# One feature multiply per tile on GpSimd instead of three on two engines, with VectorE's order fixed by the plan

## The chip, the cores and the metric

One core of one Trainium2 chip. The time is device microseconds (us) of one execution; a kernel's figure is the median of its runs. Engines are named as in the profile: PE is TensorE, DVE is VectorE, ACT is ScalarE, POOL is GpSimd, SP is the engine that issues the DMAs. Each profile is of a single execution.

All runs are called fast by the rule used here (not over 1.5% above the fastest of the same kernel). Inside that there are two groups for the kernel before: in the three sets of experiments 11 of its 33 runs took 276.15 to 276.73 us, ten of them with a mean granted PE clock of 0.994, the rest about 274.1 us. In the second set six of the eleven were of the longer kind, so that its median for the kernel before is 276.15 us. Where a few tenths matter I compare medians of runs with a clock of 0.999 or 1.0, and lengths inside the traces.

## The reference, cut to what matters

```python
def reference(A_x, A_wqkv, A_w_phi, A_wo, B_x, B_w1, B_w3, B_w2):   # x: 1 x 2048 x 640, bf16
    xn = _layernorm(A_x)                                            # H = 32 heads of 20
    return A_x + _A_ref(xn, ...) + _B_ref(xn, ...)

# _A_ref: linear attention. phi of q and of k is the pair of soft maxima of +p and -p:
    pk = jnp.einsum("bhsd,hdf->bhsf", k, w_phi)
    phi_k = jnp.concatenate([_softmax(pk), _softmax(-pk)], axis=-1)   # the same for q
    kv = einsum(phi_k, v);  num = einsum(phi_q, kv);  den = einsum(phi_q, sum of phi_k)
    out = (num / den) @ wo
# _B_ref: gated MLP, (silu(x w1) * (x w3)) w2, with 1536 hidden columns
```

## The kernel before

The 2048 rows are 16 tiles of 128. A tile of keys or queries becomes features in four steps: PE projects, ACT takes the exponentials of +p and -p (1280 numbers per row), DVE sums each head's 20 numbers and takes 64 reciprocals, and then the exponentials are multiplied by them into `phi`. The 32 heads are laid out in 11 blocks of three, so the last block has two heads. The kernel before multiplies the ten full blocks on POOL, one instruction for each sign, and the two heads left over on DVE:

```python
        def red():                                     # DVE: sums per head
            nc.vector.reduce_sum(out=box["s"]..., in_=box["e"]..., axis=AX.X)
        def rec():                                     # DVE: 64 reciprocals
            nc.vector.reciprocal(out=box["r"][:], in_=box["s"][:])
        n = HB * (NB - 1)                              # 30 of the 32 heads
        def tail():                                    # DVE: the last two heads, 80 numbers
            pinned[key, t] = nc.vector.tensor_mul(out=box["phi"][:, NB - 1, :, 0 : 2 * Dh]..., 
                in0=box["e"][:, :, n * Dh : D]..., in1=box["r"][:, :, n:H, None].to_broadcast(...))
        for sgn, eng in enumerate(engines):            # POOL, twice 600 numbers
            def mul(sgn=sgn, eng=eng): ...
```

All work is first entered in a `Plan`, a list scheduler in Python with a guessed duration for each operation. It puts the operations in order of their planned start. In the kernel before, the instructions are then handed over in that order, but the scheduler of the tile framework may still reorder them on each engine. Two things tie it down: the DMA queue is chained, and "pins" place the layer norm's statistics and applies on DVE behind a named instruction:

```python
    for h in parts:
        ins = nc.vector.bn_stats(out=stats[:, t, h, :], in_=xg[c][:, i, ...])
        if k is not None:
            order_after(ins, pinned[k])
```

The gated MLP runs in the gaps: for each of 48 groups PE does two sets of five 128x512 matmuls into PSUM banks (six in the ring), ACT takes `th = tanh(gate/2)`, DVE forms `gs = (th + 1) * gate`, ACT copies `up`, POOL multiplies `hT = gs * up`. A gate bank is free for PE again only when DVE has done `gs`.

The softmax here doesn't subtract the row's maximum and nothing guards it: scores larger than these inputs give would overflow.

## Time and profile before

274.14 us, median of 5 (273.95 to 274.28).

| what | value | where read |
|---|---|---|
| span of the trace | 272.6 us | page |
| PE busy | 264.4 us, 97% | page |
| PE waits in the middle | 0.80, 0.52, 0.76, 0.94 us | timeline of PE |
| DVE busy | 184.7 us, 68% | page |
| small multiplies on DVE | 32, together 27.8 us | groups by form |

The head of the page of the kernel before: span, then for each engine busy time, share and number of instructions.

```profile
span 272.6 us, 5218 instructions
...
PE 264.4 (97%) x1964; PEld 163.8 (60%) x1964; DVE 184.7 (68%) x347; ACT 127.0 (47%) x285; POOL 138.9 (51%) x154
...
```

PE is busy 97% of the time, so little is left to win: 8 us, and the start and the end own some of that. The list of waits of PE (who waited, for whom: total us, times, longest):

```profile
...
PE bank L633 <- DVE gs L654: 2.1, 3, 0.8
PE bank L432 <- DMA wv<-in_A_wqkv_dram: 1.2, 1, 1.2
PE kva L562 <- DVE phi L517: 0.9, 1, 0.9
...
PE bank L406 <- DVE xn L339: 0.3, 1, 0.3
```

The first and third lines are the ones a change in the middle of the kernel can win. The table of windows in four stretches of 10 us (busy time and count of PE, PE weight loads, DVE, ACT, POOL; then clock, DMA share, GB/s):

```profile
...
40.00:50.00 10.00, 9.20 (x56) 4.64 (x55) 9.90 (x16) 5.80 (x13) 8.27 (x8) 1.00 0.84 229
50.00:60.00 10.00, 9.48 (x78) 5.59 (x77) 8.42 (x17) 6.21 (x14) 9.67 (x10) 1.00 0.30 101
...
90.00:100.00 10.00, 10.00 (x86) 6.77 (x85) 10.00 (x12) 7.37 (x20) 6.42 (x6) 1.00 0.01 2
100.00:110.00 10.00, 9.24 (x66) 5.50 (x64) 10.00 (x11) 6.66 (x17) 7.62 (x7) 1.00 0.65 196
...
```

DVE is full in two of the stretches where PE stops for it, 40:50 and 100:110. But it is as full in 90:100, where PE does not stop, and in 50:60, where PE stops at 53.3 us, it is busy for only 8.42 of 10 us. So a full DVE alone does not tell where PE stops. The groups by form (output and inputs, shapes, count, then busy us and mean ns of one), first of DVE, then of POOL:

```profile
...
L507 DVE TENSOR_TENSOR phi<-eq,qr 128x80 bf16<-128x80 bf16 x16 | 15.0, 939 | 0.2
...
L339 DVE TENSOR_SCALAR xn<-xg,mv,rstd 128x640 bf16<-128x640 bf16 x16 | 12.8, 806 | 0.1
L507 DVE TENSOR_TENSOR phi<-ek,kr 128x80 bf16<-128x80 bf16 x16 | 12.8, 799 | 0.3
...
```

```profile
...
L517 POOL TENSOR_TENSOR phi<-eq,qr 128x600 bf16<-128x600 bf16 x32 | 37.8, 1203 | 23.7 <-DVE qr L501 18.7 <-issue 2.5 <-ACT eq L481 2.4
...
```

An 80-element multiply at 0.80 to 0.94 us is dear beside a 600-element one at 1.2 us on POOL.

### The profile page before, as it was taken

The numbers are of one execution on the slowest core, as the hardware profiler recorded it, in microseconds if no ns is written. First come the engines' busy times: TensorE is split into PE (matmuls) and PEld (weight loads), VectorE is DVE, ScalarE is ACT, GpSimd is POOL, SyncE is SP. The second block draws the span as 40 slices with busy tenths as digits, with TensorE's granted clock in tenths as the row PEclk, the third lists the DMA queues.
The fourth block names the chain that finished last, engine by engine and source line by source line (L and its number), as shares of the span: only waits on it lengthen the run. The fifth ranks groups of instructions, "written<-read, shape, count | busy, mean of one in ns | idle before, by whom it ended". The sixth has DMA issues, their size and how long they took to land.

```text
span 272.6 us, 5218 instructions
## 1 busy us (share of the span) xinstructions
PE 264.4 (97%) x1964; PEld 163.8 (60%) x1964; DVE 184.7 (68%) x347; ACT 127.0 (47%) x285; POOL 138.9 (51%) x154
## 2 busy tenths in 40 slices
PE   7999999899999998999989999999999999999996
PEld 2545555455555665666645577766665765657775
DVE  5525899976866999799997828876567563444321
ACT  3668676557667776677754404233234133121000
POOL 6133567994568576988885422434632553112000
PEclk9999999999999999999999999999999999999999
DMA  7999917700260016706169456299815747312241
GB/s 199 311 246 296 269 52 176 266 2 0 96 99 0 2 54 180 216 24 173 69 165 333 111 140 167 103 230 277 209 49 140 173 145 202 101 51 63 83 73 48
DMA packets 70265, 38.11 MB, mean 140 GB/s; under 512 B 49632, under 2 KB 68192, under 8 KB 70240
## 3 DMA queue, kind: packets, MB, share of 16 engines
q1 hardware_dynamic: 69664, 37.42, 51.1%
q10 hardware_dynamic: 576, 0.36, 0.5%
q8 instruction: 15, 0.25, 0.4%
q14 instruction: 10, 0.08, 0.1%
HBM read 12.81 MB, written 12.98 MB: 95 GB/s over the span
## 4 chain that ended last, share of the span: by engine, by line
PE 77%; DVE 13%; issue 4%; DMA 2%; ACT 2%; SPq 0%; ACTq 0%; DVEq 0%
PE bank L633 30%; PE bank L798 19%; PE bank L432 16%; PE bank L811 8%; DVE xn L339 2%; DVE ks L490 2%; DVE phi L507 2%; DMA wv<-in_A_wqkv_dram 2%; PE rtbank L708 2%; DVE gs L654 2%; DVE qs L490 2%; DVE stats L294 1%; PE bank L590 1%; DVE kr L501 1%; ACT ek L481 1%
## 5 line engine op out<-in xcount | busy, mean ns | idle before, releaser
L633 PE MATMUL bank<-xnT,w 128*128 128x512 bf16 x480 | 110.1, 379 | 2.1 <-DVE gs L654 2.1
L677 POOL TENSOR_TENSOR hT<-gs,up 128x512 bf16<-128x512 bf16 x48 | 56.1, 1171 | 77.1 <-DVE gs L654 35.2
L633 PEld LDWEIGHTS <-w 128*128 128x128 bf16 x480 | 46.4, 98 | 52.4 <-issue 2.8
L432 PEld LDWEIGHTS <-xnT 128*128 128x128 bf16 x480 | 45.8, 98 | 21.3 <-issue 1.2
L798 PE MATMUL bank<-w,hT 128*128 128x320 bf16 (+2 forms) x396 | 55.0, 295 | 0.0
L517 POOL TENSOR_TENSOR phi<-eq,qr 128x600 bf16<-128x600 bf16 x32 | 37.8, 1203 | 23.7 <-DVE qr L501 18.7
L798 PEld LDWEIGHTS <-hT 128*128 128x128 bf16 x396 | 38.2, 98 | 15.6
L649 ACT ACTIVATE th<-bank 128x512 bf16<-128x512 f32 x48 | 28.7, 599 | 39.8 <-PE bank L633 39.8
L654 DVE SCALAR_TENSOR_TENSOR gs<-th,bank 128x512 bf16<-128x512 bf16 x48 | 32.5, 678 | 19.7 <-ACT th L649 19.2
L481 ACT ACTIVATE eq<-bank 128x320 bf16<-128x320 f32 x64 | 22.9, 439 | 44.1 <-PE bank L432 33.7
L672 ACT ACTIVATE up<-bank 128x512 bf16<-128x512 f32 x48 | 28.7, 597 | 24.9 <-PE bank L633 24.9
L517 POOL TENSOR_TENSOR phi<-ek,kr 128x600 bf16<-128x600 bf16 x31 | 37.0, 1213 | 0.0
L490 DVE TENSOR_REDUCE qs<-eq 128x64 f32<-128x1280 bf16 x16 | 23.7, 1482 | 12.0 <-ACT eq L481 12.0
L490 DVE TENSOR_REDUCE ks<-ek 128x64 f32<-128x1280 bf16 x16 | 23.6, 1472 | 8.7 <-ACT ek L481 8.7
L432 PE MATMUL bank<-wv,xnT 128*128 128x320 bf16 x160 | 24.7, 299 | 1.3 <-DMA wv<-in_A_wqkv_dram 1.2
L811 PE MATMUL bank<-wo,oT 128*128 128x320 bf16 (+2 forms) x165 | 24.6, 294 | 0.0
L432 PE MATMUL bank<-wkphi,xnT 128*128 128x320 bf16 x160 | 24.3, 299 | 0.0
L432 PE MATMUL bank<-wqphi,xnT 128*128 128x320 bf16 x160 | 24.3, 299 | 0.0
L737 DVE TENSOR_SCALAR den<-rtbank 128x18 f32<-128x18 f32 (+1 forms) x32 | 4.9, 173 | 27.8 <-PE rtbank L708 27.8
L481 ACT ACTIVATE ek<-bank 128x320 bf16<-128x320 f32 x64 | 23.0, 439 | 0.6 <-PE bank L432 0.4
L825 DVE TENSOR_TENSOR res<-bank,xr 128x320 bf16<-128x320 f32 (+2 forms) x33 | 14.5, 470 | 10.4 <-PE bank L811 10.4
L811 PEld LDWEIGHTS <-oT 128*128 128x128 bf16 x165 | 14.9, 97 | 4.9
(55 smaller groups left out, 188.1 us busy)
## 6 DMA issues: line engine op xcount, KB each, us to landing
pqd<-phi SPq DMA_DIRECT2D x16, 352.0 KB, 2.7
w<-in_B_w_dram SPq DMA_DIRECT2D x8, 480.0 KB, 7.0
xr<-in_A_x_dram SPq DMA_DIRECT2D x4, 640.0 KB, 6.9
od<-om SPq DMA_DIRECT2D x16, 160.0 KB, 2.5
out_dram<-res SPq DMA_DIRECT2D x15, 160.0 KB, 2.3
xnd<-xn SPq DMA_DIRECT2D x3, 640.0 KB, 3.2
w<-in_B_w_dram SPq DMA_DIRECT2D x1, 1920.0 KB, 8.4
xg<-in_A_x_dram SPq DMA_DIRECT2D x9, 160.0 KB, 3.5
```

Source lines behind the costliest of these rows:

```text
L432: nc.tensor.matmul(o["ps"][:], xnT[:, c, t * P : (t + 1) * P], w[:, c, 320 * half : 320 * half + 320], start=(c == 0), stop=(c == KD - 1),)
L481: nc.scalar.activation(out=box["e"][:, sgn, 320 * half : 320 * half + 320], in_=o["ps"][:], func=AF.Exp, scale=1.0 - 2.0 * sgn,)
L490: nc.vector.reduce_sum(out=box["s"][:].rearrange("p a h -> p (a h)"), in_=box["e"][:].rearrange("p a (h d) -> p (a h) d", d=Dh), axis=AX.X,)
L517: (nc.vector if eng == "DVE" else nc.gpsimd).tensor_mul(out=box["phi"][:, 0 : NB - 1, sgn, 0 : HB * Dh].rearrange("p b (h d) -> p b h d", ...
L633: nc.tensor.matmul(o["ps"][:], w[:, k, fi * P : (fi + 1) * P], xs[:, k, :], start=(k == 0), stop=(k == KD - 1))
L649: nc.scalar.activation(out=box["th"][:], in_=og["ps"][:], func=AF.Tanh, scale=0.5)
L654: pinned["g", c, fi] = nc.vector.scalar_tensor_tensor(out=box["gs"][:], in0=box["th"][:], scalar=1.0, in1=og["ps"][:], op0=ALU.add, op1=AL ...
L672: nc.scalar.activation(out=box["up"][:], in_=ou["ps"][:], func=AF.Copy, scale=0.5)
L677: lambda: nc.gpsimd.tensor_mul(out=hT[c][:, fi, :], in0=box["gs"][:], in1=box["up"][:]),
L798: nc.tensor.matmul(o["ps"][:], hT[c][:, fi, ti * P : (ti + 1) * P], w2[:, fi, lo:hi], start=(fi == 0), stop=False,)
L811: nc.tensor.matmul(o["ps"][:], oT[c][:, k, ti * P : (ti + 1) * P], wo_of[0][:, k, lo:hi], start=False, stop=(k == KD - 1),)
L825: nc.vector.tensor_tensor(out=box["res"][:, lo:hi], in0=o["ps"][:], in1=xr[c][:, ti, lo:hi], op=ALU.add)
```

## The change

Its intent: take work off DVE, let the plan know that DVE and POOL can block each other, and make DVE follow the plan exactly.

- Exponentials and reciprocals get padded buffers with zeros (33 heads instead of 32), so one POOL instruction of 1320 elements makes a whole `phi`; the small DVE multiply is gone. Key tiles 14 and 15 are multiplied wholly on DVE.
- The plan gets a shared `port`: POOL's operations and some of DVE's queue behind one another in it.
- The pins go; DVE and SP (not PE, ACT and POOL) are held to the planned order (`manual_schedule`).
- Query tile 6 moves between the last two key accumulations; read-outs and residual loads move a little; five warm-up matmuls in place of two at one point.
- Some guesses of the plan change as well: the second block of x is expected at 24.5 instead of 19 us, some durations differ, and `gs` and a few others get a head start (`soon`).

The diff, cut to its core:

```diff
+            done = (max(t, port) if o["port"] else t) + o["dur"]        # Plan.run
+            if o["port"]:
+                port = done
...
+    exps = [acts.tile([P, 2, HB * NB, Dh], bf, name=f"exp{i}") for i in range(4)]
+    recs = [acts.tile([P, 2, HB * NB], f32, name=f"rec{i}") for i in range(2)]
...
-        muls.append(plan.op("DVE", dve_us(2 * (H - n) * Dh), tail, deps=[last, pa], frees=[ea]))
-        for sgn, eng in enumerate(engines): ...                      # two of 600 on POOL
+        if engines == ("DVE", "DVE"):
+            muls = [plan.op("DVE", dve_us(1320), mul(0, 2, nc.vector), ..., port=True)]
+        elif engines[1] == "POOL":
+            muls = [plan.op("POOL", 2.5, mul(0, 2, nc.gpsimd), deps=[last, pa], frees=[ea])]
...
-        ... features(t, "k", ("POOL", "POOL" if t < NST - 1 else "DVE"))
+        ... features(t, "k", ("POOL", "POOL") if t < NST - 2 else ("DVE", "DVE"))
...
-                if k is not None:
-                    order_after(ins, pinned[k])
...
-    plan.op("PE", 0.4, lambda: dummies(2))
+    plan.op("PE", 0.4, lambda: dummies(5))
...
-        if 8 <= t < 15:
+        if 8 <= t < 14:
             Q(t - 8)
     KV(NST - 2)
+    Q(6)
...
-    for o in order: ... order_after(ins, queued)                     # SP only
+    with tc.manual_schedule(engines={ET.SP, ET.DVE}):
+        for o in order:
+            if o["n"] >= early:
+                o["fn"]()
```

More of the change, by code (lines that the diff above doesn't have):

```diff
@@ L17, in __init__, with op @@
         self.ops = []
-    def op(self, eng, dur, fn, deps=(), takes=None, frees=(), after=0.0, lat=0.0, soon=0.0):
+    def op(self, eng, dur, fn, deps=(), takes=None, frees=(), after=0.0, lat=0.0, soon=0.0, port=False):
         o = dict(eng=eng, dur=dur, fn=fn, deps=[d for d in deps if d is not None], takes=takes,
-                 frees=list(frees), after=after, lat=lat, soon=soon, n=len(self.ops), end=None, open=0)
+                 frees=list(frees), after=after, lat=lat, soon=soon, port=port or eng == "POOL", n=len(self.ops), end=None, open=0)
         for f in o["frees"]:
@@ L36, in run @@
         left = len(self.ops)
+        port = 0.0
         def ready(o):
@@ L66, in run @@
                 ring.remove(min(ring))
-            o["start"], o["end"] = t, t + o["dur"] + o["lat"]
-            free[o["eng"]] = t + o["dur"]
+            done = (max(t, port) if o["port"] else t) + o["dur"]
+            if o["port"]:
+                port = done
+            o["start"], o["end"] = t, done + o["lat"]
+            free[o["eng"]] = done
             queue[o["eng"]].remove(o)
@@ L247, in kv_constants @@
             nc.gpsimd.memset(phi[:, :, :, HB * Dh : 64], 0.0)
-            nc.gpsimd.memset(phi[:, NB - 1, :, 2 * Dh : HB * Dh], 0.0)
+        for e in exps:
+            nc.gpsimd.memset(e[:, :, H:, :], 0.0)
+        for r in recs:
+            nc.gpsimd.memset(r[:, :, H:], 0.0)
         for q in range(2):
@@ L253, in kv_constants @@
         )
-    pinned = {}
     pin_of = {}
-    def order_after(ins, other):
-        tc.add_manual_dep(
-            ins.ins, other.ins.name,
-            mybir.DependencyInfo(mybir.DependencyClass.NoSync, mybir.DependencyReason.DATA), reason="order",
-        )
     plan = Plan(dict(bank=6, five=4, half=2, pair=4, phi=5, om=4, kv=2, th=3, gs=3, up=3, hT=3, big=3))
@@ L277 @@
     rstd = consts.tile([P, NST], f32, name="rstd")
-    arrive = [2.2, 2.6, 3.0, 3.4] + [19.0] * 4
+    arrive = [2.2, 2.6, 3.0, 3.4] + [24.5] * 4
     stats_of = {}
@@ L293, in fn @@
             for h in parts:
-                ins = nc.vector.bn_stats(out=stats[:, t, h, :], in_=xg[c][:, i, h * 320 : (h + 1) * 320])
-                if k is not None:
-                    order_after(ins, pinned[k])
+                nc.vector.bn_stats(out=stats[:, t, h, :], in_=xg[c][:, i, h * 320 : (h + 1) * 320])
             if parts[-1] == 1:
@@ L338, in fn @@
         def fn():
-            ins = nc.vector.tensor_scalar(
+            nc.vector.tensor_scalar(
                 out=xn[c][:, i, :], in0=xg[c][:, i, :], scalar1=mv[:, t, 0:1], scalar2=rstd[:, t : t + 1],
@@ L342, in fn @@
             )
-            if k is not None:
-                order_after(ins, pinned[k])
-        apply_of[t] = plan.op("DVE", 0.5, fn, deps=[rstd_of[t], *deps], frees=[xg_of[c]])
+        apply_of[t] = plan.op(
+            "DVE", dve_us(D, 4), fn, deps=[rstd_of[t], *deps], frees=[xg_of[c]], port=True, soon=1.5 if c == 1 else 0.0
+        )
         return apply_of[t]
@@ L369, in LN_out @@
             "SP", 0.5,
-            lambda: [nc.sync.dma_start(out=xn_d[c][:].rearrange("(t p) d -> p t d", p=P), in_=xn[c][:])],
+            lambda: nc.sync.dma_start(out=xn_d[c][:].rearrange("(t p) d -> p t d", p=P), in_=xn[c][:]),
             deps=ds, frees=[a], lat=3.5,
@@ L374, in tr @@
         def tr():
-            pinned["xnT", c] = ins = nc.sync.dma_start_transpose(
+            nc.sync.dma_start_transpose(
                 out=xnT[:, :, 512 * c : 512 * c + 512], in_=xn_d[c][:]
             )
-            return [ins]
         xt = plan.op("SP", 2.5, tr, deps=[st], lat=3.0)
@@ L462, in features @@
         box = {}
-        exps = []
+        done = []
         w, ready = (wkphi, wphi_ready["k"]) if key == "k" else (wqphi, wphi_ready["q"])
         def al():
-            box["e"] = work.tile([P, 2, D], bf, name="e" + key, tag="pair", bufs=4)
+            box["e"] = exps.pop(0)
+            exps.append(box["e"])
         def alp():
@@ L481, in ex @@
                     nc.scalar.activation(
-                        out=box["e"][:, sgn, 320 * half : 320 * half + 320], in_=o["ps"][:],
-                        func=AF.Exp, scale=1.0 - 2.0 * sgn,
+                        out=box["e"][:, sgn, 16 * half : 16 * half + 16, :],
+                        in_=o["ps"][:].rearrange("p (h d) -> p h d", d=Dh), func=AF.Exp, scale=1.0 - 2.0 * sgn,
                     )
-                exps.append(plan.op("ACT", act_us(320), ex, deps=[u, ea], frees=[u]))
+                done.append(plan.op("ACT", act_us(320), ex, deps=[u, ea], frees=[u]))
@@ L488, in red @@
         def red():
             box["s"] = small.tile([P, 2, H], f32, name=key + "s", tag="ks", bufs=2)
-            nc.vector.reduce_sum(
-                out=box["s"][:].rearrange("p a h -> p (a h)"),
-                in_=box["e"][:].rearrange("p a (h d) -> p (a h) d", d=Dh), axis=AX.X,
-            )
-        last = plan.op("DVE", dve_us(2 * D), red, deps=exps)
-        pa = plan.alloc("phi", alp)
-        muls = []
-        def rec():
-            box["r"] = small.tile([P, 2, H], f32, name=key + "r", tag="kr", bufs=2)
-            nc.vector.reciprocal(out=box["r"][:], in_=box["s"][:])
@@ L503, in features @@
-        last = plan.op("DVE", dve_us(2 * H, 0.15), rec, deps=[last])
-        n = HB * (NB - 1)
-        def tail():
-            pinned[key, t] = nc.vector.tensor_mul(
-                out=box["phi"][:, NB - 1, :, 0 : 2 * Dh].rearrange("p a (h d) -> p a h d", d=Dh),
-                in0=box["e"][:, :, n * Dh : D].rearrange("p a (h d) -> p a h d", d=Dh),
-                in1=box["r"][:, :, n:H, None].to_broadcast([P, 2, H - n, Dh]),
-            )
-        muls.append(plan.op("DVE", dve_us(2 * (H - n) * Dh), tail, deps=[last, pa], frees=[ea]))
@@ L514, in features @@
-        for sgn, eng in enumerate(engines):
-            def mul(sgn=sgn, eng=eng):
-                (nc.vector if eng == "DVE" else nc.gpsimd).tensor_mul(
-                    out=box["phi"][:, 0 : NB - 1, sgn, 0 : HB * Dh].rearrange("p b (h d) -> p b h d", d=Dh),
-                    in0=box["e"][:, sgn, 0 : n * Dh].rearrange("p (b h d) -> p b h d", h=HB, d=Dh),
-                    in1=box["r"][:, sgn, 0:n, None]
-                    .to_broadcast([P, n, Dh])
-                    .rearrange("p (b h) d -> p b h d", h=HB),
-                )
-            muls.append(
-                plan.op(eng, dve_us(n * Dh) if eng == "DVE" else 1.22, mul, deps=[last, pa], frees=[ea])
-            )
+            nc.vector.reduce_sum(out=box["s"][:], in_=box["e"][:, :, 0:H, :], axis=AX.X)
@@ new lines, in features, with rec, mul, fn @@
+        last = plan.op("DVE", dve_us(2 * D), red, deps=done)
+        def rec():
+            box["r"] = recs.pop(0)
+            recs.append(box["r"])
+            nc.vector.reciprocal(out=box["r"][:, :, 0:H], in_=box["s"][:])
+        last = pin_of[key, t] = plan.op("DVE", dve_us(2 * H, 0.15), rec, deps=[last])
+        pa = plan.alloc("phi", alp)
+        def mul(at, n, eng):
+            def fn():
+                eng.tensor_mul(
+                    out=box["phi"][:, :, at : at + n, 0 : HB * Dh].rearrange("p b a f -> p a b f"),
+                    in0=box["e"][:, at : at + n].rearrange("p a (b h) d -> p a b (h d)", h=HB),
+                    in1=box["r"][:, at : at + n, :, None].to_broadcast([P, n, HB * NB, Dh]),
+                )
+            return fn
@@ new lines, in features @@
+        if engines == ("DVE", "DVE"):
+            muls = [plan.op("DVE", dve_us(1320), mul(0, 2, nc.vector), deps=[last, pa], frees=[ea], port=True)]
+        elif engines[1] == "POOL":
+            muls = [plan.op("POOL", 2.5, mul(0, 2, nc.gpsimd), deps=[last, pa], frees=[ea])]
+        else:
+            muls = [
+                plan.op("POOL", 1.3, mul(0, 1, nc.gpsimd), deps=[last, pa], frees=[ea]),
+                plan.op("DVE", dve_us(660), mul(1, 1, nc.vector), deps=[last, pa], frees=[ea], port=True),
+            ]
@@ L528, in features @@
         return muls, pa, box
     def K(t):
-        phik_of[t], phik_a[t], _ = features(t, "k", ("POOL", "POOL" if t < NST - 1 else "DVE"))
-        pin_of["k", t] = phik_of[t][0]
+        phik_of[t], phik_a[t], _ = features(t, "k", ("POOL", "POOL") if t < NST - 2 else ("DVE", "DVE"))
     def Q(t, engines=("POOL", "POOL")):
@@ L567, in fn @@
                 )
-        KV_of[t] = plan.op("PE", pe_us(NB, 63), fn, deps=phik_of[t] + V_of[t], frees=[phik_a[t]])
+        KV_of[t] = plan.op("PE", 0.032 * NB, fn, deps=phik_of[t] + V_of[t], frees=[phik_a[t]])
     FSPANS = (
@@ L653, in gs @@
         def gs():
-            pinned["g", c, fi] = nc.vector.scalar_tensor_tensor(
+            nc.vector.scalar_tensor_tensor(
                 out=box["gs"][:], in0=box["th"][:], scalar=1.0, in1=og["ps"][:], op0=ALU.add, op1=ALU.mult
             )
-        b = plan.op("DVE", dve_us(512), gs, deps=[a, ab["gs"]], frees=[ug, ab["th"]])
+        b = plan.op("DVE", dve_us(512), gs, deps=[a, ab["gs"]], frees=[ug, ab["th"]], soon=0.4)
         pin_of["g", c, fi] = b
@@ L692, in fn @@
                 )
-            kvm_of.append(plan.op("DVE", dve_us(63 * (b1 - b0)), fn, deps=[KV_of[NST - 1]]))
+            kvm_of.append(plan.op("DVE", dve_us(63 * (b1 - b0)), fn, deps=[KV_of[NST - 1]], soon=1.0))
     rt_of = {}
@@ L714, in RT @@
             u = plan.op(
-                "PE", pe_us(b1 - b0, 63), fn, deps=[kvm_of[half], pqT_of[pair]], takes="kv", frees=[pqT_a[pair]]
+                "PE", 0.032 * (b1 - b0), fn, deps=[kvm_of[half], pqT_of[pair]], takes="kv", frees=[pqT_a[pair]]
             )
@@ L946 @@
     for t in range(4, 8):
-        ln_stats(t, ("g", 0, t - 2))
+        ln_stats(t)
     wq_seq = prep("q", wqT, wqphi, 34.0)
@@ L989 @@
             gates[0][0]()
+        if t < 2:
+            RT(t + 3)
+            ATT(t + 3)
+            OT(t + 3)
+        if t == 0:
             gates[1][0]()
@@ L992 @@
             gates[t][0]()
-        if t + 3 < NST:
-            if t % 4 == 1:
-                residual(t // 4 + 1)
-            RT(t + 3)
-            ATT(t + 3)
-            OT(t + 3)
         gates[t][1]()
@@ L1001 @@
             Q(t + 8)
+        if t % 4 == 3 and t < NST - 1:
+            residual(t // 4 + 1)
+        for n in (t + 3,) if 1 < t < 9 else (t + 4,) if 8 < t < 12 else ():
+            RT(n)
+            ATT(n)
+            OT(n)
         if 3 <= t < 11:
             fill(1.5 * 2.16)
+        if t == 8:
+            RT(12)
+            ATT(12)
+            OT(12)
         if t == 10:
@@ L1014 @@
     kv_constants()
-    queued = None
-    for o in order:
-        if o["n"] >= early:
-            ins = o["fn"]()
-            if o["eng"] == "SP":
-                for ins in ins:
-                    if queued is not None:
-                        order_after(ins, queued)
-                    queued = ins
+    with tc.manual_schedule(engines={ET.SP, ET.DVE}):
+        for o in order:
+            if o["n"] >= early:
+                o["fn"]()
     kvpool.release()
```

## The prediction

> **What bounds the kernel now.** The tensor engine. The page's busy table gives PE 264.4 us of a 272.6 us span (97%) at a granted clock of 1.0; in the timeline of PE the groups stand back to back at their own pace (ten 128x512 matmuls every 2.16 us, ten 128x320 every 1.36 us). What PE does not use, from its list of waits and timeline: about 0.8 us at the start, 0.3 us for the first normalised tile, 1.2 us for the value weights' DMA (6.0 to 7.2 us), a tail of some 2.8 us after the last matmul, and four stalls in the middle: 0.80 us at 48.1, 0.52 at 53.3, 0.76 at 106.6 (all three: DVE gs, which frees PSUM banks) and 0.94 at 142.3 (the last key tile's phi, multiplied on DVE behind POOL). Counted from when the next matmul could have been issued, these four cost about 0.96 + 0.68 + 0.92 + 1.10 = 3.7 us. DVE is full (9.9 to 10 of 10 us, table of windows) just in 40:50 and 90:110, so there it is DVE that stops PE.
>
> **What the change does.**
> - It drops 32 small DVE multiplies (phi, 128x80). Lines by form: 15.0 + 12.8 = 27.8 us, 0.87 us each, though one that ran with POOL idle took 0.24 us. The Trainium skill, "SBUF — State Buffer", section "Who interferes with whom", says that a DVE instruction with two SBUF inputs contends with a GpSimd instruction that reads SBUF; the trace agrees (0.24 against 0.90 to 1.24 us).
> - POOL does one 1320-element multiply per tile in place of two of 600 (2.36 us the pair). Estimate from these: 2.5 to 2.7 us. POOL had 49% idle time, so this should not reach PE. The longer single instruction makes an xn apply (0.39 us alone, 0.81 mean, up to 1.32) wait up to 2.6 us when it falls on it; the plan now places those around POOL.
> - Key tiles 14 and 15 go wholly to DVE: some 1.5 us each (estimate from the 128x512 DVE form), against 1.78 us in before, of which most was waiting.
> - Query tile 6 moves between the last two key accumulations, so PE has another 1.4 us of work during the wait of 142.3.
> - DVE follows the planned order exactly, without the pins. Small moves of the attention read-outs, residual loads and three more warm-up matmuls (0.22 us each), which fit the 1.2 us wait for the value weights and cost nothing.
> PE's needed work is unchanged.
>
> **On the critical path.** Only the 3.7 us of stalls. DVE's busy time falls by some 23 to 27 us, but it is off the path outside those stretches. The start, the weights' DMA and the tail stay. Floor: 274.1 − 3.7 = 270.4 us. I expect most of it, with about half a microsecond of new stalls from the fixed DVE order (an instruction at the head that waits for late data now holds up those behind it).
>
> **Prediction: 271.0 us, range 270.2 to 273.0.** Faster by over 2% (under 268.7) is below the floor: 0.01. Within 2%: 0.95. Slower by over 2%: 0.04.
>
> **Right or wrong in the profile.** PE busy stays 264 to 266 us; waits of PE for DVE drop from 3.0 us to under 1; DVE busy falls from 184.7 to about 160; no 128x80 phi line; POOL phi at 2.5 to 2.7 us a piece, POOL busy near 140; the DMA wait for the value weights of similar end (7.2 us).
>
> **What would make it wrong.** A DVE order that is wrong for real arrival times (second x block, residual reload of 4.4 to 8.7 us landing, now issued later), stalling gs and so PE's banks; POOL's 1320-element form slower per element, which delays phi; a changed PE order by the scheduler.

## More of the kernel before

The timeline of the kernel before around the first stall (start, length, engine, what; in brackets the idle time before it and who ended it):

```profile
...
45.82 2.32 PE L633 MATMUL bank<-xnT,w 128*128 128x512 bf16 x10
46.03 0.55 DVE L501 RECIPROCAL kr<-ks 128x64 f32<-128x64 f32 x1
46.26 1.16 POOL L677 TENSOR_TENSOR hT<-gs,up 128x512 bf16<-128x512 bf16 x1 [0.90 <-DVE gs L654]
46.61 0.90 DVE L507 TENSOR_TENSOR phi<-ek,kr 128x80 bf16<-128x80 bf16 x1
47.10 0.60 ACT L649 ACTIVATE th<-bank 128x512 bf16<-128x512 f32 x1 [0.31 <-PE bank L633]
...
47.43 0.87 DVE L294 BATCH_NORM_STATS2 stats<-xg 128x6 f32<-128x320 bf16 x2
48.23 0.66 DVE L654 SCALAR_TENSOR_TENSOR gs<-th,bank 128x512 bf16<-128x512 bf16 x1
...
48.94 0.59 PE L633 MATMUL bank<-xnT,w 128*128 128x512 bf16 x2 [0.80 <-DVE gs L654]
...
```

Read it from the bottom. PE starts its next gate group at 48.94, when `gs` (48.23) frees a bank. `th`, which `gs` needs, was there at 47.70. In between DVE did the rest of the small multiply (46.61 to 47.51, held up by POOL's `hT` multiply, 46.26 to 47.42) and the statistics of a later tile (47.43 to 48.30), which nobody needed yet.

## The result

270.8 us, median of 7 runs (270.39 to 271.16), against 274.21 us of 13 runs of the kernel before. The ratio is 0.987 (95%: 0.985 to 0.989); ratios here are the mean time of one kernel's fast runs over that of the other's of the same rounds, so not quite the ratio of the medians. The time is inside the predicted range and within 2% of before. The profiled run was a short one, 270.12 us with a span of 268.4 us.

The same views of the kernel after: the head of its page, then the list of waits of PE.

```profile
span 268.4 us, 5127 instructions
...
PE 264.0 (98%) x1967; PEld 164.3 (61%) x1967; DVE 166.7 (62%) x316; ACT 127.2 (47%) x285; POOL 136.8 (51%) x122
...
```

```profile
...
PE bank L226 <- PEq L1033: 0.8, 1, 0.8
PE bank L431 <- DMA wv<-in_A_wqkv_dram: 0.3, 1, 0.3
PE bank L405 <- POOL band L213: 0.3, 1, 0.3
```

All four waits in the middle are gone. What is left is the start. The same four windows:

```profile
...
40.00:50.00 10.00, 10.00 (x71) 5.25 (x70) 8.53 (x15) 6.00 (x13) 9.34 (x7) 1.00 0.93 262
50.00:60.00 10.00, 10.00 (x77) 5.82 (x74) 6.20 (x13) 7.05 (x16) 9.13 (x7) 1.00 0.01 2
...
90.00:100.00 10.00, 10.00 (x73) 6.13 (x71) 9.00 (x9) 7.53 (x20) 6.39 (x4) 1.00 0.14 49
100.00:110.00 10.00, 10.00 (x75) 6.16 (x73) 8.18 (x10) 6.91 (x16) 8.40 (x6) 1.00 0.55 156
...
```

PE is full in each, and DVE is no longer. The groups of DVE and of POOL that took the place of those shown:

```profile
...
L339 DVE TENSOR_SCALAR xn<-xg,mv,rstd 128x640 bf16<-128x640 bf16 x16 | 13.4, 855 | 0.1
...
L504 DVE TENSOR_TENSOR phi<-exp,rec 128x1320 bf16<-128x1320 bf16 x2 | 4.9, 2430 | 0.2
...
```

```profile
...
L504 POOL TENSOR_TENSOR phi<-exp,rec 128x1320 bf16<-128x1320 bf16 x30 | 72.8, 2430 | 18.7 <-ACT exp L481 9.4 <-DVE rec L497 8.0 <-ACT vaug L445 0.8
...
```

POOL's one multiply takes 2.43 us, where the two took 2.4 us together. But DVE also takes 2.43 us for the same shape. The timeline of the kernel after shows why:

```profile
...
130.53 1.16 POOL L669 TENSOR_TENSOR hT<-gs,up 128x512 bf16<-128x512 bf16 x1
...
130.64 2.44 DVE L504 TENSOR_TENSOR phi<-exp,rec 128x1320 bf16<-128x1320 bf16 x1
...
135.74 1.16 POOL L669 TENSOR_TENSOR hT<-gs,up 128x512 bf16<-128x512 bf16 x1 [4.05 <-ACT up L664]
135.86 2.42 DVE L504 TENSOR_TENSOR phi<-exp,rec 128x1320 bf16<-128x1320 bf16 x1
...
```

Each DVE multiply began 0.1 us after a POOL multiply and ended 1.4 us after that one's end (which came at 131.69 and 136.90; the DVE multiplies ended at 133.08 and 138.28). So it waited for about a microsecond. This agrees with what the Trainium skill states in "SBUF — State Buffer", section "Who interferes with whom", of a DVE instruction with two SBUF inputs and a POOL instruction that reads SBUF. In another run below, with POOL idle, the same multiply took 1.53 us.

One measure of the experiments needs a word. The start of the kernel varies between runs with the arrival of its first weights: the first gate matmul begins at 13.9 to 15.2 us in the traces. From that matmul's start to the end of PE's last one, in the timeline of PE, the kernel before takes 269.42 + 0.44 − 14.46 = 255.40 us and the kernel after 265.25 + 0.44 − 13.93 = 251.76 us. The difference, 3.64 us, is what the four stalls cost (I had put them at 3.7 us). I call this length the PE stretch; it leaves out the start.

### The profile page after: what moved, and what is told of

The parts are those of the page before. It is cut to its first block, busy times and chain, and to the rows that moved or that the text cites. A ratio compares the mean times of both kernels' runs of the same rounds, so it can differ in the third digit from the quotient of the medians.

```text
span 268.4 us, 5127 instructions
## 1 busy us (share of the span) xinstructions
PE 264.0 (98%) x1967; PEld 164.3 (61%) x1967; DVE 166.7 (62%) x316; ACT 127.2 (47%) x285; POOL 136.8 (51%) x122
## 4 chain that ended last, share of the span: by engine, by line
PE 95%; DMA 2%; SPq 1%; DVE 0%; ACT 0%; issue 0%
PE bank L625 39%; PE bank L431 23%; PE bank L790 19%; PE bank L803 8%; DMA xg<-in_A_x_dram 2%; PE rtbank L700 2%; PE bank L582 1%; PE kva L554 1%; PE kvb L554 1%; SPq L174 0%; PE bank L405 0%; ACT xnT L417 0%; DVE stats L296 0%; DVE xn L339 0%; SPq L186 0%
## 5 line engine op out<-in xcount | busy, mean ns | idle before, releaser
L504 POOL TENSOR_TENSOR phi<-exp,rec 128x1320 bf16<-128x1320 bf16 x30 | 72.8, 2430 | 18.7 <-ACT exp L481 9.4
L481 ACT ACTIVATE exp<-bank 128x320 bf16<-128x320 f32 x128 | 45.7, 436 | 43.5 <-PE bank L431 43.3
L790 PEld LDWEIGHTS <-hT 128*128 128x128 bf16 x396 | 37.9, 98 | 15.2
L817 DVE TENSOR_TENSOR res<-bank,xr 128x320 bf16<-128x320 f32 (+2 forms) x33 | 15.8, 478 | 38.6 <-PE bank L803 38.6
L490 DVE TENSOR_REDUCE ks<-exp 128x64 f32<-128x1280 bf16 x16 | 23.4, 1465 | 12.3 <-ACT exp L481 12.3
L490 DVE TENSOR_REDUCE qs<-exp 128x64 f32<-128x1280 bf16 x16 | 23.7, 1479 | 5.7 <-ACT exp L481 5.7
L803 PEld LDWEIGHTS <-oT 128*128 128x128 bf16 x165 | 15.8, 98 | 5.8
L296 DVE BATCH_NORM_STATS2 stats<-xg 128x6 f32<-128x320 bf16 x32 | 13.8, 468 | 2.5 <-DMA xg<-in_A_x_dram 2.5
L445 ACT CAST vaug<-bank 128x320 bf16<-128x320 f32 x32 | 13.3, 432 | 3.2 <-PE bank L431 2.8
L339 DVE TENSOR_SCALAR xn<-xg,mv,rstd 128x640 bf16<-128x640 bf16 x16 | 13.4, 855 | 0.1
```

What stands on the lines that cost most here:

```text
L481: nc.scalar.activation(out=box["e"][:, sgn, 16 * half : 16 * half + 16, :], in_=o["ps"][:].rearrange("p (h d) -> p h d", d=Dh), func=AF.Ex ...
L490: nc.vector.reduce_sum(out=box["s"][:], in_=box["e"][:, :, 0:H, :], axis=AX.X)
L504: eng.tensor_mul(out=box["phi"][:, :, at : at + n, 0 : HB * Dh].rearrange("p b a f -> p a b f"), in0=box["e"][:, at : at + n].rearrange("p ...
L790: nc.tensor.matmul(o["ps"][:], hT[c][:, fi, ti * P : (ti + 1) * P], w2[:, fi, lo:hi], start=(fi == 0), stop=False,)
L803: nc.tensor.matmul(o["ps"][:], oT[c][:, k, ti * P : (ti + 1) * P], wo_of[0][:, k, lo:hi], start=False, stop=(k == KD - 1),)
L817: nc.vector.tensor_tensor(out=box["res"][:, lo:hi], in0=o["ps"][:], in1=xr[c][:, ti, lo:hi], op=ALU.add)
```

## The experiments

The first theory (relief) was the one that the prediction had put in front: the dropped multiplies free DVE time, and that is what PE had been short of. The rival (order): DVE had enough time, but used it in the wrong order. Each kernel below is correct and was timed in 5 rounds. The first four ran together, as did the second and the third four. What follows rests on differences under 2%: on repeated times at full clock and on lengths inside the traces.

| run | what it is | median us | PE stretch us |
|---|---|---|---|
| (before) | | 274.1 | 255.40 |
| b_tail_pool | before, small multiply on POOL | 272.03 | 253.27 |
| b_order | before, planned DVE order, no pins | 271.03 | 252.23 |
| a_tail_dve | after, small multiply back on DVE, plan told of the port | 275.04 | 256.27 |
| a_dve_auto | after, DVE order left to the scheduler | 286.51 | not comparable |
| a_q6_back | after, query tile 6 in its old place | 271.65 | 252.40 |
| a_k_back | after, key tiles 14, 15 off DVE | 270.70 | 251.75 |
| a_tail_k_back | a_tail_dve and a_k_back together | 276.95 | 257.73 |
| a_dve_load | after, more DVE work added | 271.94 | 252.96 |
| a_tail_noport | a_tail_dve, plan not told of the port | 270.96 | 251.96 |
| a_pins | after, DVE order as before: scheduler with pins | 270.74 | 251.77 |
| a_dummies2 | after, two warm-up matmuls | 270.38 | 251.75 |
| after_again | after, unchanged | 270.79 | 251.75 |

### The relief alone: b_tail_pool

```diff
-            pinned[key, t] = nc.vector.tensor_mul(      # the 128x80 multiply
+            nc.gpsimd.tensor_mul(                       # the pin goes to the reciprocal
...
-        muls.append(plan.op("DVE", dve_us(2 * (H - n) * Dh), tail, ...))
+        muls.append(plan.op("POOL", 0.3, tail, ...))
```

> The kernel before, with only the small 128x80 multiply moved from DVE to POOL (PE's order unchanged, DVE's almost). Theory R (relief: DVE's time at the port stopped PE): the three PE stalls on gs (2.1 us by the waits) shrink to under 0.5 us, DVE busy falls by 20 us or more, and with the stall on the last key tile untouched the time is about 271.5 to 272.3 us. Rival O (order: the pins put DVE's work in a bad order, the planned order is what helped): two or three gs stalls stay, time 273.5 to 274.3 us.

Measured: 272.03 us, all gs waits gone, DVE busy 158.8 us. One wait in the middle is left in its list of waits of PE, for the last key tile, now finished by POOL:

```profile
...
PE kva L561 <- POOL phi L517: 1.3, 1, 1.3
...
```

So relief is enough against the gs stalls. That is as the prediction had it.

### The order alone: b_order

```diff
-            order_after(ins, pinned[k])                 # all pins off
-    for o in order: ... order_after(ins, queued)
+    with tc.manual_schedule(engines={ET.SP, ET.DVE}):
+        for o in order: ...
```

> The kernel before, with DVE and SP held to the planned order and the pins gone, but all multiplies as before (PE's order unchanged). Theory R: the gs stalls stay within 1 us of their 2.1 us, or grow, time 273 to 275 us. Rival O: they vanish, time about 271.5 to 272.3 us. Both leave the stall of some 0.9 us at the last key tile.

Measured: 271.03 us, a gain of 3.1 us, with every multiply where it was and PE's order unchanged. DVE is busy 178.1 us, only 6.6 us less than before, and in 40:50 it is as full as it was (9.93 of 10 us). The rival was right, and it did more than either theory said: the wait for the last key tile is gone as well. The timeline at the place of the first stall:

```profile
...
45.59 0.96 DVE L504 TENSOR_TENSOR phi<-ek,kr 128x80 bf16<-128x80 bf16 x1
...
46.47 0.67 DVE L651 SCALAR_TENSOR_TENSOR gs<-th,bank 128x512 bf16<-128x512 bf16 x1
47.02 0.60 ACT L646 ACTIVATE th<-bank 128x512 bf16<-128x512 f32 x1 [0.31 <-PE bank L630]
47.07 0.87 DVE L291 BATCH_NORM_STATS2 stats<-xg 128x6 f32<-128x320 bf16 x2
47.20 2.10 PE L630 MATMUL bank<-xnT,w 128*128 128x512 bf16 x9 [0.21 <-DVE gs L651]
...
```

`gs` now comes before the statistics of the later tile, and PE loses 0.21 us instead of 0.80. The small multiplies are there too, but they meet POOL less often: their means are 0.69 and 0.59 us, against 0.94 and 0.80 before.

### Undoing the relief: a_tail_dve, a_tail_k_back, a_tail_noport

The edit of all three puts the 128x80 multiply back on DVE and two of 600 on POOL, in a planned order. a_tail_dve gives the small multiply `port=True` in the plan:

```diff
-            muls = [plan.op("POOL", 2.5, mul(0, 2, nc.gpsimd), ...)]
+            muls = [plan.op("DVE", dve_us(2 * (H - n) * Dh), tail, ..., port=True)]
+            for sgn in range(2):
+                muls.append(plan.op("POOL", 1.22, part, ...))
```

> The kernel after, with the phi multiply split again: the 128x80 end on DVE, two of 600 on POOL; the planned DVE order and all the rest kept. Theory R: DVE busy rises by some 18 us, PE waits for DVE gs by 1 us or more again, time 271.8 to 273.5 us. Rival O: no PE stall over 0.3 us comes back, time within 0.4 us of the kernel after (270.8).

Measured: 275.04 us, slower than either theory said, and even than the kernel before. No wait for gs returned, but these, in the list of waits of PE:

```profile
...
PE kva L576 <- DVE phi L505: 2.1, 2, 1.7
PE bank L825 <- DMA oT<-od: 1.8, 2, 1.0
...
```

The timeline of DVE before the longest of them:

```profile
...
132.61 1.48 DVE L491 TENSOR_REDUCE ks<-exp 128x64 f32<-128x1280 bf16 x1
135.82 0.69 DVE L668 SCALAR_TENSOR_TENSOR gs<-th,bank 128x512 bf16<-128x512 bf16 x1 [1.74 <-ACT th L663]
136.43 0.55 DVE L498 RECIPROCAL rec<-qs 128x64 f32<-128x64 f32 x1
...
138.12 2.53 DVE L505 TENSOR_TENSOR phi<-exp,rec 128x1320 bf16<-128x1320 bf16 x1
...
142.81 1.53 DVE L505 TENSOR_TENSOR phi<-exp,rec 128x1320 bf16<-128x1320 bf16 x1
...
```

From 134.09 to 135.82 DVE sat idle. `gs` stood next in the fixed order and waited for `th`, while two reciprocals, whose sums were done, stood behind it. Then the big multiply had to wait for POOL's (2.53 us; the later one found POOL idle and took 1.53 us), and PE waited for both. The next run took the big multiplies off DVE again:

```diff
-        ... features(t, "k", ("POOL", "POOL") if t < NST - 2 else ("DVE", "DVE"))
+        ... features(t, "k", ("POOL", "POOL") if t < NST - 1 else ("POOL", "DVE"))
```

> The kernel after with the small multiplies back on DVE (which took 275.04 us) and the last two key tiles back on POOL and half POOL, half DVE. If what cost 4 us there was the 1320-element DVE multiplies standing behind a full DVE: the PE waits of 1.7 and 0.4 us for phi go, time 270.8 to 272.3 us. Rival (the small multiplies themselves hold up PE, wherever the last tiles go): time over 273.5 us.

Measured: 276.95 us. The guess about the big multiplies fell: the wait moved to POOL and grew to 4.25 us. The idle gap of DVE before gs was still there (its `gs` at 134.98 had waited 1.74 us). It also cost clock. Its table of windows, one us each (PE is the first pair, the clock stands before the last two numbers):

```profile
...
141.00:142.00 1.00, 0.00 (x0) 0.00 (x0) 1.00 (x2) 0.00 (x0) 1.00 (x1) 1.00 0.37 144
142.00:143.00 1.00, 0.36 (x7) 0.36 (x8) 0.92 (x1) 0.00 (x0) 1.00 (x2) 0.81 0.00 0
143.00:144.00 1.00, 1.00 (x10) 0.48 (x8) 0.00 (x0) 0.00 (x0) 0.85 (x1) 0.50 0.38 88
145.00:146.00 1.00, 1.00 (x14) 0.72 (x13) 0.55 (x2) 0.60 (x1) 0.00 (x0) 0.50 1.28 291
146.00:147.00 1.00, 1.00 (x6) 0.43 (x5) 0.97 (x3) 0.00 (x0) 0.00 (x0) 0.98 1.04 150
...
```

PE had stopped at 138.4; from 143 to 146 its granted clock was half. All six runs had a mean clock of 0.994 or less. The Trainium skill, "TensorE: Matmul & The Clock Gate", Part 1, says that the clock is halved after at least one idle window of about 3.4 us; a gap of 4.25 us did it here, and the half clock lasted about as long as such a window (some 3.4 us by the table).

What was left as the suspect was the order that the plan had made of `port=True`. So that was taken away, and only that, from a_tail_dve:

```diff
-            muls = [plan.op("DVE", dve_us(2 * (H - n) * Dh), tail, ..., port=True)]
+            muls = [plan.op("DVE", dve_us(2 * (H - n) * Dh), tail, ...)]
```

> The kernel after with the small multiplies back on DVE as in the run that took 275.04 us, except that the plan is not told that they wait for POOL. The planned DVE order then puts them elsewhere, as in the run of the kernel before with the planned order (271.03 us), where most took 0.23 us. If it is the place in DVE's order that makes them dear: their mean falls from 0.83 us to under 0.7, the waits of 1.7 us and of oT go, time 270.8 to 271.8 us. Rival (small multiplies plus two big DVE multiplies are too much for DVE in any order): time over 273 us.

("Most took 0.23 us" is not right: in the trace of b_order 14 of the 32 took 0.22 to 0.24 us, the others up to 1.27 us.)

Measured: 270.96 us, no wait of PE in the middle. The page's line of engines and the group of small multiplies, by form:

```profile
...
PE 263.1 (98%) x1941; PEld 164.3 (61%) x1967; DVE 184.4 (69%) x346; ACT 127.2 (47%) x285; POOL 135.9 (51%) x157
...
```

```profile
...
L519 DVE TENSOR_TENSOR phi<-exp,rec 128x80 bf16<-128x80 bf16 x30 | 21.0, 704 | 0.7
...
```

DVE is as busy as in the kernel before (184.4 and 184.7 us), the small multiply costs 0.70 us a piece (just missing the expected "under 0.7"), and the PE stretch is 251.96 us, 0.2 us from the best. DVE is also full where it was full before (9.83, 10.00 and 9.90 of 10 us in 40:50, 90:100 and 100:110), and PE does not stop. So the 4 us of a_tail_dve were an order, not the multiplies. They were not DVE's order alone, though. PE is not held to the plan, and the traces show that the flag changed its order too: in a_tail_dve and a_tail_k_back the second-last key accumulation (key tile 14, the one that waits longest) comes after query tile 6, in a_tail_noport before it, as in the kernel after. No run parts the two. In b_order and a_pins the order of PE and of ACT is unchanged, so those two do speak of DVE's order.

### Undoing the order: a_dve_auto, a_pins

```diff
-    with tc.manual_schedule(engines={ET.SP, ET.DVE}):
+    with tc.manual_schedule(engines={ET.SP}):
```

> The kernel after, with DVE's order left to the scheduler again and no pins (PE's, ACT's and SP's orders are the same as in the kernel after). Theory R: DVE has room, so any sane order will do: PE stalls under 0.5 us, time within 0.5 us of 270.8. Rival O: stalls come back, time over 271.8 us.

Measured: 286.51 us. The reason lies at the very start, and neither theory had it. With no pins and no fixed order the scheduler put statistics of the second block of x in front of the first block's last ones. The timeline of DVE:

```profile
...
20.93 1.28 DVE L296 BATCH_NORM_STATS2 stats<-xg 128x6 f32<-128x320 bf16 x3 [11.39 <-DMA xg<-in_A_x_dram]
...
```

DVE stood for 11.4 us before a DMA, PE for 13.9 us behind it, and PE's clock was at half after. In the rest of this run PE waits 0.67 us for gs once. So the run says what a missing pin costs (about 15.7 us against the kernel after, together with the half clock), not whether the kernel needs the planned order. The clean version restores the pins:

```diff
+                if k is not None:
+                    order_after(ins, pinned[k])         # statistics and applies, as before
-    with tc.manual_schedule(engines={ET.SP, ET.DVE}):
+    with tc.manual_schedule(engines={ET.SP}):
```

> The kernel after with DVE's order left to the scheduler, but held by the pins of the kernel before (the run without pins took 286.51 us, 13.9 us of it a PE wait at the start). PE's order is that of the kernel after. Relief alone is enough (as moving the small multiply to POOL was for the gs waits): no PE wait on gs over 0.3 us, time 270.6 to 271.5 us. If the planned order is needed even with the multiply gone: PE waits of 1 us and more on gs, time over 271.8 us.

Measured: 270.74 us, PE stretch 251.77 us, no wait in the middle. With the multiply gone, the old way of ordering is good enough.

### More load on DVE: a_dve_load

```diff
+        def extra():                                    # result unused
+            idle = small.tile([P, H], f32, name="idle", tag="idle", bufs=2)
+            nc.vector.reduce_sum(out=idle[:], in_=box["e"][:, 0, 0:H, :], axis=AX.X)
+        plan.op("DVE", dve_us(D), extra, deps=[last], frees=[ea])
```

> The kernel after, with one more sum of 640 elements on DVE per tile, of one operand from SBUF[...]; its result is not used. About 0.82 us each, 26 us in all, as much as the dropped multiplies. If DVE's time as such is what PE runs short of: PE waits of 1 us and more on gs or phi come back, time 272 to 275 us. Rival (only collisions with POOL or a bad order cost PE time; in a planned order DVE has room): no wait over 0.3 us, time within 0.5 us of 270.8.

Measured: 271.94 us. The added sums did not wait for POOL: they took 0.75 to 0.81 us each, though a POOL instruction ran beside 31 of the 32. DVE is busy 185.2 us, and PE waits 0.97 us, but only once, for the phi of key tile 14 (the second-last); none for gs. This lies between the theories. The amount of DVE work of the kernel before, in a planned order, does not bring back the gs stalls; at the key tiles that are multiplied on DVE it costs 1.2 us of PE stretch. Here too PE's order changed, as in a_tail_dve: key tile 14's accumulation comes after query tile 6.

### The smaller parts: a_q6_back, a_k_back, a_dummies2, and the control

```diff
# a_q6_back
-        if 8 <= t < 14:
+        if 8 <= t < 15:
             Q(t - 8)
-    Q(6)
# a_k_back
-        ... ("POOL", "POOL") if t < NST - 2 else ("DVE", "DVE")
+        ... ("POOL", "POOL" if t < NST - 1 else "DVE")
# a_dummies2
-    plan.op("PE", 0.4, lambda: dummies(5))
+    plan.op("PE", 0.4, lambda: dummies(2))
```

> The kernel after, with query tile 6 back in its old place (before the second-last key accumulation). The prediction held that this move fills the wait of 142 us: then PE waits for the last key tile's phi by some 0.5 to 1 us again, time 271.3 to 271.8 us. Rival, since the planned order alone (271.03 us) had lost that wait too: no such wait, time within 0.4 us of 270.8.

Measured: 271.65 us, PE stretch 252.40 us, a wait of 0.47 us for the last key tile. The move of query tile 6 is worth 0.6 us, beside the key tiles on DVE.

> The kernel after, with key tile 14 multiplied on POOL and key tile 15 half on POOL, half on DVE, in place of both whole on DVE. If that move is what ended the wait for the last key tile: a wait of 0.5 to 1 us there, time 271.3 to 271.8 us. Rival (the order, or query tile 6 between, is enough): no wait, time within 0.4 us of 270.8.

Measured: 270.70 us, PE stretch 251.75 us. Putting key tiles 14 and 15 on DVE is worth nothing as long as query tile 6 stands between.

> The kernel after with two warm-up matmuls in place of five. The prediction held that the three more cost nothing and bring nothing: same time as the kernel after within 0.3 us, granted clock 1.0. If they keep the clock up: some runs with a granted clock under 0.996 and a time 2 us longer.

Measured: 270.38 us (270.15 to 270.78), clock 0.999 or 1.0, PE stretch 251.75 us. The extra warm-up matmuls bring nothing. The median is 0.4 us under the control's, more than the 0.3 us expected, but the ranges overlap and the difference lies in the start, which varies; I don't claim a gain.

> The kernel after, unchanged, as the control of these rounds: 270.4 to 271.2 us, all runs at a granted clock of 0.999 or 1.0.

Measured: 270.79 us (270.07 to 271.13, so two runs just outside the expected span), clock 0.999 or 1.0.

Five traces have a PE stretch of 251.75 to 251.77 us (the kernel after twice, a_k_back, a_pins, a_dummies2). That is PE with no gap (in the kernel after it is busy for all 251.76 us), so with these matmuls nothing done on DVE or POOL can go below it. No version found beats the kernel after clearly; what remains is the start and the tail.

## Why the prediction was right or wrong

- **The ceiling: right.** PE's needed work did not change (264.4 and 264.0 us busy), so the gain could be no more than the stalls. Estimated 3.7 us, measured 3.64 us of PE stretch, and 3.4 us in the medians. The time of 271.0 us against 270.8 us measured follows from that. Any cause that ended the stalls would have given it, so the number says nothing for the mechanism below.
- **What ends the gs stalls: half right.** In the prediction the dropped multiplies are what relieves DVE, and the fixed order appears only as a cost. Dropping them is sufficient (b_tail_pool: no gs wait), but not necessary: the planned order alone does it (b_order: 0.2 us left), and with the order the same load on DVE costs 0.2 us (a_tail_noport). The weak step was "DVE is full ... so there it is DVE that stops PE", read as a lack of DVE time. A full DVE with the urgent instruction first is enough for PE (a_tail_noport: 10.00 of 10 us in 90:100, no wait). Each of the two parts gives a margin, and once one is there the other is worth little: b_order 271.03, a_pins 270.74, both together 270.8 us.
- **The fixed order: wrong in sign.** The prediction listed it as a risk of "about half a microsecond of new stalls from the fixed DVE order". No new stall came with it; in the kernel before it gained 3.1 us, and once the multiplies are gone it gains nothing (a_pins). The danger named was real, but showed only with another plan: in a_tail_dve and a_tail_k_back the head of DVE's queue waited 1.7 us for late data with ready work behind it.
- **The wait at 142 us: right, with redundancy.** The query tile's move fills it (a_q6_back loses 0.6 us). But the planned order had ended it by itself in b_order, and the move of the key tiles to DVE did nothing.
- **The big DVE multiply: mis-sized.** Estimated at "some 1.5 us each", measured 2.44 and 2.42 us, as each met a POOL multiply; with POOL idle it took 1.53 us. The contention with POOL that the prediction had named for the small multiplies was forgotten for the big ones. It cost PE nothing.
- **DVE's busy time: mis-sized.** "About 160" was 166.7 us. Counts times means of DVE's groups fall from 204.1 to 179.7 us, 24.4 us, as estimated (23 to 27). But in a dense queue the records of neighbours overlap by some 0.08 us, and busy time counts that once: it fell only by 18.0 us.
- **POOL, apply, warm-up matmuls: right.** POOL's multiply took 2.43 us (2.5 to 2.7 expected; a little under), an apply took up to 2.54 us, its wait included (the prediction: a wait of up to 2.6), and the warm-up matmuls do nothing. The first-weights wait did not end at a "similar" time: the first projection began at 7.17 us before and 6.38 us after, and between 6.4 and 7.6 us in the traces of the experiments. This is variation of the arrival, not the change, and it is why this profiled run was short.

Left open: why a third of the runs of the kernel before took about 2.4 us longer at a mean clock of 0.994. None of the 14 runs of the kernel after did; one of the six of b_tail_pool did (274.23 us). A mean of 0.994 is also what a_tail_k_back shows, with about 3.4 us at half clock in its trace, so these runs may have had one such stretch. That is an estimate: no profile fell on such a run.

## What to carry to other kernels

When the profile shows a full engine in front of the one that bounds the kernel, ask first what stands ahead of the urgent instruction in its queue: with the same instructions, order alone can be worth as much as taking some of them away (here 3.1 us against 2.1 us). Two changes that each nearly suffice hide one another, so a change made of both must be tested with each part alone, not only with each part undone. And a fixed order is only as good as the durations it was planned with; one more constraint in the plan (the port flag on the small multiply, though that multiply does wait for POOL) made the kernel 0.9 us slower than before, with a waiting instruction at the head of DVE's queue.

## What the Trainium skill lacked or had wrong

- "SBUF — State Buffer", section "Who interferes with whom": confirmed, and the wait goes both ways. The 1320-element DVE multiply took 1.51 to 1.53 us with POOL idle and, over all traces, 1.99 to 3.48 us behind POOL's; with DVE's in between, two POOL multiplies took 3.65 us instead of 2.36 us. What the page has no figure for is how far placing the instruction shortens the wait: the mean of the same 80-element multiply went from 0.94 and 0.80 us to 0.69 and 0.59 us by order alone.
- "GPSIMD Engine Reference", section "3.1 Elementwise — side-by-side cycle accounting", gives about 2.6 cycles an element for a POOL two-input operation on fp32 (4497 ns for 2048). For bf16 times a broadcast fp32 operand, these runs show 1203 ns for 600 and 2430 ns for 1320 elements: 1.70 ns for each further element, an estimate of 2.0 cycles at the page's 1.2 GHz (the access patterns of the two differ). That is less than the 2.6. The page has no figure for such a form.
- "TensorE: Matmul & The Clock Gate", Part 1: nothing to correct. The traces agree: half clock after PE gaps of 4.25 us and 13.9 us, and none after gaps of up to 1.7 us.
- In none of the pages did I find a figure for what the order in an engine's queue can be worth with the same instructions (here 3.1 us of 274).
